# Spectral block with 128-row x2 tiles, column tiles for 64-row leftovers, merged stores, a reordered tail and shared copies of v

## The chip, the cores and the metric

The kernel runs on one core of one Trainium2 chip. The metric is device time in microseconds (us), taken from the execution on the chip; lower is better.

Names used below: PE is TensorE's matmul, PEld its weight load, DVE VectorE, ACT ScalarE, POOL GpSimd, SP SyncE, which only issues DMAs here. "L785" is line 785 of the kernel that the profile belongs to. The lines move between versions, so the tile names (out, num, x, dft, qpt) are what to hold on to.

## The reference

Two blocks in a row, batch 8, 576 positions, 8 heads of 64. The first is a linear attention with a cosine reweighting; the second projects to three branches, filters one of them along the sequence with a Fourier transform, gates, and projects back:

```python
def _attn_ref(q, k, v):                 # 8 x 8 x 576 x 64 each
    c, s = cos(pi/2 * pos/S), sin(pi/2 * pos/S)
    q_p = concat([relu(q)*c, relu(q)*s]);  k_p = concat([relu(k)*c, relu(k)*s])
    kv  = einsum('bhsf,bhsd->bhfd', k_p, v);  z = k_p.sum(axis=2)
    num = einsum('bhsf,bhfd->bhsd', q_p, kv)
    den = einsum('bhsf,bhf->bhs', q_p, z)[..., None] + 1e-06
    return num / den

def _moe_ref(x, w_proj, filter_fft, w_out):        # x: 8 x 576 x 512
    x1, x2, x3 = split(x @ w_proj, 3)
    y = x1 * irfft(rfft(x2, axis=1) * rfft(filter_fft, axis=0), n=S, axis=1) * x3
    return y @ w_out                               # 8 x 576 x 512, float32
```

(cut and shortened; `...` calls are numpy's.)

## The kernel before

It handles one batch after the other, software-pipelined: while PE finishes batch b's spectral part, DVE and ACT prepare batch b+1's q and k.

The projection x2 and the forward transform work in blocks of 96 rows:

```python
def emit_x2(b, bls=range(3)):
    ...
    for bl in bls:
        u = unit(f"x2_{b}_{bl}")
        for comp in range(2):
            for c in range(NC):                      # NC = 4
                nc.tensor.matmul(u[0:NP, comp],      # NP = 96
                    fx[:, c, ds(comp * 6 + 2 * bl, 2)].rearrange("p a b -> p (a b)"),
                    wp16[:, c, ds(DM, DM)], start=(c == 0), stop=(c == NC - 1))
        mark["x2f", b, bl] = nc.scalar.mul(out=x2f[:, bl], in_=u[0:NP], mul=X2SC)
# emit_dft: one matmul per (bl, comp) against tre / tim
```

The output has 576 rows in an order of 12 groups of 48: row k of group r lies at DRAM row 12k + r. It is computed in five tiles of 128 rows, and each piece of at most 48 rows of one group is one store, nearly all of them on SP's queue:

```python
OT = [0, 128, 256, 384, 448]
def emit_out(b, grps=OG):
    ov = out[b].rearrange("(k r) n -> r k n", r=12)
    ...
            while pos < hi_:
                m = pos // 48
                e = min(hi_, (m + 1) * 48)
                k0 = pos - m * 48
                r = 6 * (m % 2) + m // 2
                q_ = nc.sync
                if m % 2 == 1 and (last or (b == B - 2 and t > 1)):
                    q_ = nc.scalar if last else nc.gpsimd
                q_.dma_start(out=ov[r, k0 : k0 + e - pos], in_=sv[pos - OT[t] : e - OT[t]])
                pos = e
```

SP's queue also carries two kinds of DMA transpose: qp into qpt, which the matmul num uses as weights, and att into xt, which the gate matmuls of the spectral block use.

## Time and profile before

| | before |
|---|---|
| time, median of the 4 runs beside the changed kernel | 252.69 us (252.07 to 259.23) |
| profiled span | 252.0 us |
| start of the first of six full out groups | 90.53 us |
| five periods from there, to the last out start at 215.47 | 124.9 us |
| from there to the end | 36.5 us |

### The profile page before, as it was taken

Reading aid. Unit: us, or ns where it says so; the run is one execution under the profiler, and the core shown is the slowest. Engines: PE = TensorE matmul, PEld = TensorE weight load, DVE = VectorE, ACT = ScalarE, POOL = GpSimd, SP = SyncE. Lnnn points to the kernel's source line nnn. Section 1 sums busy time; section 2 is a strip of 40 time slices with the busy share of each in tenths; the row PEclk is TensorE's granted clock in tenths of the full one; section 3 lists DMA queues with packets and bytes.
Section 4 is the critical chain, followed back from the end, with each engine's and each line's share of the span. In section 5 each row is a group of like instructions: output and inputs, shape, how many; then the busy total and the mean of one; then the engine's idle time right before and its main releaser. Section 6 shows DMA issues by size and latency. Waiting matters only on the chain.

```text
span 252.0 us, 6140 instructions
## 1 busy us (share of the span) xinstructions
PE 226.1 (90%) x2313; PEld 159.9 (63%) x2313; DVE 210.4 (83%) x732; ACT 186.2 (74%) x281; POOL 38.1 (15%) x65
## 2 busy tenths in 40 slices
PE   0197897998988999999999999999999999999980
PEld 0067575655676867686768676867686778557730
DVE  7689899699779999999799979997998595828880
ACT  2244789799797876987698769876987488767720
POOL 8714211501501031103110311000000000000030
PEclk9997998899799999999999999999999999999996
DMA  5999999799999969999999999999982512153054
GB/s 68 167 205 205 207 200 153 101 166 196 173 121 157 169 56 202 174 176 194 200 225 143 141 217 199 137 183 156 161 197 53 153 41 58 44 146 83 3 153 140
DMA packets 74926, 37.30 MB, mean 148 GB/s; under 512 B 54288, under 2 KB 70160, under 8 KB 74896
## 3 DMA queue, kind: packets, MB, share of 16 engines
q0 software_dynamic: 26176, 17.21, 51.3%
q1 hardware_dynamic: 48320, 19.11, 40.6%
q10 hardware_dynamic: 400, 0.59, 0.7%
q8 instruction: 18, 0.29, 0.5%
q14 instruction: 12, 0.10, 0.2%
HBM read 33.69 MB, written 9.44 MB: 171 GB/s over the span
## 4 chain that ended last, share of the span: by engine, by line
PE 73%; DVE 13%; ACT 7%; DMA 3%; issue 1%; POOL 1%; POOLq 0%; DVEq 0%; ACTq 0%
PE x L674 21%; PE x L634 17%; PE out L752 12%; PE kv L527 5%; PE num L568 4%; PE fx L595 4%; PE dft L649 3%; DMA vraw<-in_v_dram 3%; PE inv L711 2%; PE inv L710 2%; DVE kp L104 2%; ACT va L142 1%; DVE eo L725 1%; DVE att L578 1%; PE qt L547 1%
## 5 line engine op out<-in xcount | busy, mean ns | idle before, releaser
L674 PE MATMUL x<-xt,wp 128*128 128x288 f16 x512 | 68.1, 286 | 0.0
L674 PEld LDWEIGHTS <-wp 128*128 128x128 f16 x512 | 48.9, 98 | 13.9 <-issue 0.9
L634 PE MATMUL x<-wp,fx 128*96 128x512 f16 x192 | 48.1, 395 | 1.6 <-DVE qpt L553 1.6
L752 PE MATMUL out<-wo,y 128*128 128x512 f16 x160 | 36.0, 379 | 0.1
L639 ACT ACTIVATE x2f<-x 96x1024 f16<-96x1024 f32 x24 | 24.5, 1020 | 14.2 <-PE x L634 13.9
L634 PEld LDWEIGHTS <-fx 128*96 128x96 f16 x192 | 23.0, 127 | 16.7 <-issue 3.7
L142 ACT COPY va<-vraw 96x768 f16<-96x768 f16 x32 | 25.2, 831 | 9.2 <-DMA vraw<-in_v_dram 9.2
L578 DVE TENSOR_TENSOR att<-num,rcp 96x768 f16<-96x768 f32 x32 | 30.3, 948 | 0.2
L752 PEld LDWEIGHTS <-y 128*128 128x128 f16 x160 | 15.3, 97 | 17.7 <-DVE y L730 0.6
L527 PE MATMUL kv<-va,kp 96*128 96x65 f16 x384 | 16.6, 199 | 10.2 <-ACT va L142 8.4
L684 ACT CAST x3s<-x 128x576 f16<-128x576 f32 x32 | 20.5, 641 | 5.9 <-PE x L674 5.9
L759 ACT ACTIVATE os<-out 128x1024 f32<-128x1024 f32 (+1 forms) x21 | 17.7, 880 | 9.0 <-PE out L752 8.7
L610 ACT CAST fx<-fx 128x576 f16<-128x576 f32 x32 | 20.6, 645 | 4.9 <-PE fx L595 4.9
L651 ACT CAST xf<-dft 96x1024 f16<-96x1024 f32 x24 | 24.2, 1008 | 0.0
L527 PEld LDWEIGHTS <-kp 96*128 96x128 f16 x384 | 15.1, 101 | 13.6 <-DVE kp L104 11.3
L699 DVE TENSOR_TENSOR g<-x3s,x1s 128x288 f16<-128x288 f16 x64 | 17.2, 299 | 6.8 <-ACT x3s L684 6.8
L681 ACT CAST x1s<-x 128x576 f16<-128x576 f32 x32 | 20.6, 645 | 1.8 <-PE x L674 0.8
L654 DVE TENSOR_TENSOR m<-xf,h 96x1024 f16<-96x1024 f16 x24 | 16.3, 681 | 6.1 <-ACT xf L651 5.1
L568 PEld LDWEIGHTS <-qpt 128*128 128x128 f16 (+1 forms) x384 | 16.2, 103 | 7.7 <-issue 3.9
L725 DVE TENSOR_TENSOR eo<-eq 128x288 f16<-128x288 f16 x64 | 17.5, 297 | 4.4 <-ACT eq L714 4.4
L595 PE MATMUL fx<-fm,att 96*128 96x96 f16 x240 | 17.0, 214 | 3.4 <-DVE att L578 1.7
L595 PEld LDWEIGHTS <-att 96*128 96x128 f16 x240 | 14.3, 101 | 7.6 <-DVE att L578 3.4
(192 smaller groups left out, 409.1 us busy)
## 6 DMA issues: line engine op xcount, KB each, us to landing
out_dram<-os SPq DMA_DIRECT2D x64, 96.0 KB, 2.2
kraw<-in_k_dram POOLq DMA_DIRECT2D x7, 576.0 KB, 8.6
vraw<-in_v_dram POOLq DMA_DIRECT2D x7, 576.0 KB, 8.9
qraw<-in_q_dram POOLq DMA_DIRECT2D x8, 288.0 KB, 6.0
qraw<-in_q_dram POOLq DMA_DIRECT2D x12, 144.0 KB, 5.9
wp<-in_moe_w_proj_dram POOLq DMA_DIRECT2D x3, 512.0 KB, 11.9
out_dram<-os SPq DMA_DIRECT2D x22, 64.0 KB, 2.2
out_dram<-os SPq DMA_DIRECT2D x23, 32.0 KB, 2.1
```

What stands on the lines that cost most here:

```text
L142: nc.scalar.copy(out=va_buf[b % 2][:, hs, :, 0:D], in_=raw_t[(b, "v")][:, hs].rearrange("p h (j d) -> p h j d", j=NJ),)
L527: nc.tensor.matmul(u[:, h // 4, ds((h % 4) * 65, 65)], kp[:, j, h].rearrange("p a b -> p (a b)"), va[:, h, j, 0:65], start=(j == 0), stop= ...
L568: nc.tensor.matmul(u[0:m, hh, ds(t * 65, 65)], qpt[:, c0 : c0 + 2 * m - 1 : 2], kvs[:, h // 4, ds((h % 4) * 65, 65)], start=True, stop=True,)
L578: mark["att", b, hp] = nc.vector.tensor_tensor(out=att[:, :, ds(hp * 128, 128)].rearrange("p t (h d) -> p h t d", h=2), in0=nv[:, :, :, 0: ...
L595: nc.tensor.matmul(dst.rearrange("p (g e o) -> p g e o", e=2, o=8)[:, :, e], att[:, 2 * j + e, ds(c * 128, 128)], fm[0:NP, gs], start=True ...
L610: mark["fx", b] = nc.scalar.copy(out=dst[:, c].rearrange("p g (j o) -> p j g o", j=3), in_=uf[:, 0:768].rearrange("p (j g o) -> p j g o", ...
L634: nc.tensor.matmul(u[0:NP, comp], fx[:, c, ds(comp * 6 + 2 * bl, 2)].rearrange("p a b -> p (a b)"), wp16[:, c, ds(DM, DM)], start=(c == 0) ...
L639: mark["x2f", b, bl] = nc.scalar.mul(out=x2f[:, bl], in_=u[0:NP], mul=X2SC)
L651: mark["xf", b, bl] = nc.scalar.copy(out=xf, in_=u[0:NP])
L674: nc.tensor.matmul(u[:, hf, 0:HS], wp16[:, i, ds(w * DM + c * 128, 128)], xt[:, i, ds(6 * hf, 6)].rearrange("p a b -> p (a b)") if b < DMA ...
L681: mark["x1s", b, c] = nc.scalar.copy(out=x1s, in_=us[0][:, :, 0:HS])
L752: nc.tensor.matmul(u[:, x], y[:, c, ds(OT[t], 128)], wo16[:, c], start=(c == 0), stop=(c == NC - 1),)
```

## The change

Its intent: fewer PE rows in x2 (three blocks of 96 rows and two components fit in four full tiles of 128 and a half one), the half tiles of x2 and out run as pairs of 64-column tiles side by side, two neighbouring groups of 48 output rows leave in one store of 96 rows, the last batch's work is reordered and its stores alternate between two queues, and half of the copies of v go from ACT to DVE at a later point. The core of the diff:

```diff
 # x2 and dft
-            for comp in range(2):
-                for c in range(NC):
-                    nc.tensor.matmul(u[0:NP, comp], fx[:, c, ds(comp * 6 + 2 * bl, 2)]..., ...)
+            if bl < 2:
+                for x in range(2):
+                    for c in range(NC):
+                        mm(u[:, x], 2 * bl + x, 128, c, range(NC))
+            else:
+                for c in range(2):
+                    for x in range(2):
+                        mm(u[ds(64 * x, 64), 0], 4, 64, c + 2 * x, range(2 * x, 2 * x + 2))
...
+    DFT = (
+        ((tre[:, 0], 0),), ((tpad[0], 0), (tpad[1], 1)), ((tpad[2], 1), (tpad[3], 2)),
+        ((tpad[4], 2),), ((tre[:, 2], 3),), ((tpad[5], 3), (tpad[6], 4)),
+    )
 # out
-        ov = out[b].rearrange("(k r) n -> r k n", r=12)
+        ov = out[b].rearrange("(k x y) n -> x y k n", x=2, y=6)
...
-                    e = min(hi_, (m + 1) * 48)
+                    e = pos + 96 if pos % 96 == 0 and pos + 96 <= hi_ else min(hi_, (m + 1) * 48)
                     q_ = nc.sync
-                    if m % 2 == 1 and (last or (b == B - 2 and t > 1)):
-                        q_ = nc.scalar if last else nc.gpsimd
+                    if last:
+                        q_ = (nc.sync, nc.scalar)[store[0] % 2]
+                    store[0] += 1
+                    if e - pos == 96:
+                        q_.dma_start(out=ov[:, m // 2], in_=sv[pos - OT[t] : e - OT[t]])
...
 # the loop over batches
-            for x in range(2):
-                with behind(*(("x2f", b, x) if b > 1 else ("kvs", 2))):
-                    emit_va(n + 1, (2 * x, 2 * x + 1))
+            ...
+                with behind("eo", b, 3):
+                    emit_va(n + 1, (0, 1))
+                with behind("g", b, 0):
+                    emit_va(n + 1, (2, 3), nc.vector.tensor_copy)
```

(cut: the padded tables' set-up, the 64-row tile of out, which goes as four pairs of 256-column halves, the last batch's accumulation order, the tail's order.) Three of a batch's stores become 96-row stores, 24 in all. Their place in DRAM is two runs of 48 rows.

More of the change, by code (lines that the diff above doesn't have):

```diff
@@ L83 @@
     tim = consts.tile([NP, 3, NP], FP16, tag="tim", name="tim")
+    tpad = [consts.tile([128, NP], FP16, tag=f"tpad{i}", name=f"tpad{i}") for i in range(7)]
     ire = consts.tile([NP, 4, QS], FP16, tag="ire", name="ire")
@@ L119 @@
     raw_t = {}
-    DMA_XT = 2
+    XT_DMA = (2, 3, 4, 5, 6, 7)
     DMA_QT = 2
@@ L137, in load_qk, with emit_va @@
             nc.gpsimd.dma_start(out=rw[:, hs], in_=view)
-    def emit_va(b, xs=range(4)):
+    def emit_va(b, xs=range(4), copy=nc.scalar.copy):
         for x in xs:
             hs = slice(2 * x, 2 * x + 2)
-            nc.scalar.copy(
+            copy(
                 out=va_buf[b % 2][:, hs, :, 0:D],
@@ L199, in emit_cols @@
         nc.vector.memset(warm, 0.0)
+        for t in tpad:
+            nc.vector.memset(t, 0.0)
         sj = cc["s6_i"]
@@ L279, in emit_fm @@
         nc.vector.tensor_tensor(out=ph, in0=ph, in1=rr, op=AL.subtract)
-        nc.scalar.activation(out=coef[:, 0:6], in_=ph, func=AF.Sin, scale=TWO_PI)
-        tsc(coef[:, 3:6:2], coef[:, 3:6:2], 1.0 / R3, AL.mult)
-        tsc(coef[:, 0:6], coef[:, 0:6], 2.0, AL.mult)
-        tsc(coef[:, 0:6], coef[:, 0:6], RC, AL.add, -RC, AL.add)
-        tsc(coef[:, 0:6], coef[:, 0:6], 0.5, AL.mult)
-        tsc(coef[:, 6:12], coef[:, 0:6], side, AL.mult)
+        cv = coef[:, 0:12].rearrange("p (b c s) -> p b c s", b=3, c=2)
+        c0, cb = cv[:, :, 0], cv[:, 1:3, 0, 1]
+        nc.scalar.activation(
+            out=c0, in_=ph.rearrange("p (b s) -> p b s", b=3), func=AF.Sin, scale=TWO_PI
+        )
+        tsc(cb, cb, 1.0 / R3, AL.mult)
+        tsc(c0, c0, 2.0, AL.mult)
+        tsc(c0, c0, RC, AL.add, -RC, AL.add)
+        tsc(c0, c0, 0.5, AL.mult)
+        tsc(cv[:, :, 1], c0, side, AL.mult)
         irow_i = cc["orow_i"][:, 0:6]
@@ L386, in emit_fwd_tables @@
             nc.vector.tensor_tensor(out=tb[:, 0], in0=tb[:, 0], in1=mask, op=AL.mult)
+        for i, to, tb, bl, lo, n in (
+            (0, 96, tim, 0, 0, 32), (1, 0, tim, 0, 32, 64), (2, 64, tre, 1, 0, 64),
+            (3, 0, tre, 1, 64, 32), (4, 32, tim, 1, 0, 96), (5, 96, tim, 2, 0, 32),
+            (6, 0, tim, 2, 32, 64), (6, 64, tim, 2, 32, 64),
+        ):
+            nc.sync.dma_start(out=tpad[i][to : to + n], in_=tb[lo : lo + n, bl])
     def emit_inv_turns():
@@ L588, in emit_fx @@
             fx_t[b] = work.tile([128, NC, 12, 48], FP16, tag="fx", bufs=2, name=f"fx{b}")
-            if b < DMA_XT:
+            if b not in XT_DMA:
                 xt_t[b] = work.tile([128, NC, 12, 48], FP16, tag="xt", bufs=2, name=f"xt{b}")
@@ L601, in emit_fx @@
             for dst, gs in ((fx, slice(0, 12)), (xt_t.get(b), slice(12, 24))):
-                if gs.start and b >= DMA_XT:
+                if gs.start and b in XT_DMA:
                     continue
@@ L627, in emit_x2, with mm @@
         if 0 in bls:
-            moe.setdefault(b, {})["x2f"] = work.tile([NP, 3, 2, DM], FP16, tag="x2f", name=f"x2f{b}")
+            moe.setdefault(b, {})["x2f"] = work.tile([128, 5, DM], FP16, tag="x2f", name=f"x2f{b}")
         x2f = moe[b]["x2f"]
+        def mm(dst, ch, n, c, cs):
+            nc.tensor.matmul(
+                dst, fx[:, c].rearrange("p g o -> p (g o)")[:, ds(128 * ch, n)],
+                wp16[:, c, ds(DM, DM)], start=(c == cs[0]), stop=(c == cs[-1]),
+            )
         for bl in bls:
             u = unit(f"x2_{b}_{bl}")
-            for comp in range(2):
-                for c in range(NC):
-                    nc.tensor.matmul(
-                        u[0:NP, comp],
-                        fx[:, c, ds(comp * 6 + 2 * bl, 2)].rearrange("p a b -> p (a b)"),
-                        wp16[:, c, ds(DM, DM)], start=(c == 0), stop=(c == NC - 1),
-                    )
-            mark["x2f", b, bl] = nc.scalar.mul(out=x2f[:, bl], in_=u[0:NP], mul=X2SC)
+            if bl < 2:
[6 more added lines that the diff above has]
+                        mm(u[ds(64 * x, 64), 0], 4, 64, c + 2 * x, range(2 * x, 2 * x + 2))
+            n = 2 if bl < 2 else 1
+            mark["x2f", b, bl] = nc.scalar.mul(
+                out=x2f[:, 2 * bl : 2 * bl + n], in_=u[:, 0:n], mul=X2SC
+            )
     def emit_dft(b, bls=range(3)):
@@ L647, in emit_dft @@
             u = unit(f"dft{b}_{bl}")
-            for comp, tab in ((0, tre), (1, tim)):
-                nc.tensor.matmul(u[0:NP, comp], tab[:, bl], x2f[:, bl, comp], start=True, stop=True)
+            for comp in range(2):
+                mm = DFT[2 * bl + comp]
+                for x, (tab, ch) in enumerate(mm):
+                    nc.tensor.matmul(
+                        u[0:NP, comp], tab, x2f[0 : tab.shape[0], ch],
+                        start=(x == 0), stop=(x == len(mm) - 1),
+                    )
             xf = work.tile([NP, 2, DM], FP16, tag="xf", bufs=2, name=f"xf{b}_{bl}")
@@ L659, in emit_dft @@
             mark["yf", b, bl] = nc.vector.tensor_tensor(out=yf[:, bl, 1], in0=m1[:, 1], in1=m2[:, 0], op=AL.add)
+    DFT = (
+        ((tre[:, 0], 0),), ((tpad[0], 0), (tpad[1], 1)), ((tpad[2], 1), (tpad[3], 2)),
+        ((tpad[4], 2),), ((tre[:, 2], 3),), ((tpad[5], 3), (tpad[6], 4)),
+    )
     X3_ACT = (0, 1, 2, 3)
@@ L676, in emit_gate @@
                         xt[:, i, ds(6 * hf, 6)].rearrange("p a b -> p (a b)")
-                        if b < DMA_XT else xt[:, :, i, ds(48 * hf, 48)],
+                        if b not in XT_DMA else xt[:, :, i, ds(48 * hf, 48)],
                         start=(i == 0), stop=(i == NC - 1),
@@ L687, in emit_gate @@
         for hf in range(2):
-            if b < DMA_XT:
+            if b not in XT_DMA:
                 gv = (g[:, c, 0:HS] if hf == 0 else g[:, c, HS:S][:, ::-1]).rearrange(
@@ L730, in emit_y @@
         nc.vector.tensor_tensor(out=y[:, c], in0=y[:, c], in1=g[:, c], op=AL.mult)
-    OT = [0, 128, 256, 384, 448]
+    OT = [0, 128, 256, 384, 512]
+    store = [0]
+    OGL = ((1, 0), (2, 4), (3,))
     OG = ((0, 1), (2, 3), (4,))
@@ L740, in emit_out, with mm @@
             u = unit(f"out{b}_{grp[0]}")
-            os_ = {}
+            os_, us = {}, {}
+            def mm(t, c, nr):
+                nc.tensor.matmul(
+                    us[t], y[:, c, ds(OT[t], nr)], wo16[:, c],
+                    start=(c == 0), stop=(c == NC - 1),
+                )
             for x, t in enumerate(grp):
@@ L747, in emit_out @@
                     os_[t] = late["p"].tile(
-                        [128, ng, DM], FP32, tag="osl" if last else f"os{ng}", bufs=5 if last else ng,
+                        [128, ng, DM // 2 if t == 4 and not last else DM], FP32, tag="osl" if last else f"os{ng}", bufs=5 if last else ng,
                         name=f"os{b}_{t}",
                     )
-                for c in range(NC):
-                    nc.tensor.matmul(
-                        u[:, x], y[:, c, ds(OT[t], 128)], wo16[:, c],
-                        start=(c == 0), stop=(c == NC - 1),
-                    )
-                if last:
-                    tsc(os_[t][:, 0], u[:, x], OUTSC, AL.mult)
-            if not last:
+                if t == 4 and not last:
+                    for c in range(NC):
+                        for hf in range(2):
+                            nc.tensor.matmul(
+                                u[ds(64 * hf, 64), x, 0 : DM // 2], y[:, c, 512:576],
+                                wo16[:, c, ds(hf * (DM // 2), DM // 2)],
+                                start=(c == 0), stop=(c == NC - 1),
+                            )
+                    nc.scalar.mul(
+                        out=os_[t][:, 0, 0 : DM // 2], in_=u[:, x, 0 : DM // 2], mul=OUTSC
+                    )
+                    continue
+                nr = 64 if t == 4 else 128
+                us[t] = u[0:nr, 0 if last else x]
+                part = range(NC)
+                if last and grp[0] == 1:
+                    part = range(NC - 1)
+                for c in part:
+                    mm(t, c, nr)
+                if last and len(part) == NC:
+                    nv = DM if t == 4 else DM // 2
+                    tsc(os_[t][0:nr, 0, 0:nv], us[t][:, 0:nv], OUTSC, AL.mult)
+                    if nv < DM:
+                        nc.scalar.mul(out=os_[t][0:nr, 0, nv:DM], in_=us[t][:, nv:DM], mul=OUTSC)
+            if last and grp[0] == 1:
+                for t in grp:
+                    mm(t, NC - 1, 128)
+                    tsc(os_[t][:, 0], us[t], OUTSC, AL.mult)
+            if not last and grp[0] < 4:
                 nc.scalar.mul(out=os_[grp[0]], in_=u[:, 0 : len(grp)], mul=OUTSC)
@@ L761, in emit_out @@
                 sv = os_[t][:, 0] if last else os_[grp[0]][:, x]
-                lo, hi_ = (OT[t], OT[t] + 128) if t < 4 else (512, 576)
-                pos = lo
+                pos, hi_ = (128 * t, 128 * t + 128) if t < 4 else (512, 576)
                 while pos < hi_:
-                    m = pos // 48
-                    e = min(hi_, (m + 1) * 48)
-                    k0 = pos - m * 48
-                    r = 6 * (m % 2) + m // 2
+                    m, k0 = pos // 48, pos % 48
+                    e = pos + 96 if pos % 96 == 0 and pos + 96 <= hi_ else min(hi_, (m + 1) * 48)
                     q_ = nc.sync
-                    if m % 2 == 1 and (last or (b == B - 2 and t > 1)):
-                        q_ = nc.scalar if last else nc.gpsimd
-                    q_.dma_start(out=ov[r, k0 : k0 + e - pos], in_=sv[pos - OT[t] : e - OT[t]])
+                    if last:
[3 more added lines that the diff above has]
+                        q_.dma_start(out=ov[:, m // 2], in_=sv[pos - OT[t] : e - OT[t]])
+                    elif t < 4 or last:
+                        q_.dma_start(
+                            out=ov[m % 2, m // 2, k0 : k0 + e - pos], in_=sv[pos - OT[t] : e - OT[t]]
+                        )
+                    else:
+                        for hf in range(2):
+                            q_.dma_start(
+                                out=ov[m % 2, m // 2, k0 : k0 + e - pos, ds(hf * (DM // 2), DM // 2)],
+                                in_=sv[64 * hf + pos - 512 : 64 * hf + e - 512, 0 : DM // 2],
+                            )
                     pos = e
@@ L880 @@
             emit_num(n, 3)
-            emit_xt(n)
+            if n in XT_DMA:
+                emit_xt(n)
         if b == 1:
@@ L889 @@
             emit_out(b - 1, OG[0:1])
+            emit_dft(b, (2,))
+            emit_out(b - 1, OG[1:2])
         for c in range(NC):
-            if b == B - 1 and c == NC - 1:
+            if b == B - 1 and c == 2:
                 for x in range(NC):
@@ L895 @@
                 emit_gate(b, c)
-                if c == 0:
+                if c == 0 and b < B - 1:
                     emit_dft(b, (2,))
@@ L908 @@
                 emit_qt(n + 1, x)
-            with behind("att", n, 1):
+            with behind(*("att", n, 3)):
                 emit_phi(n + 1, "k")
-            for x in range(2):
-                with behind(*(("x2f", b, x) if b > 1 else ("kvs", 2))):
-                    emit_va(n + 1, (2 * x, 2 * x + 1))
+            if b == 1:
+                with behind("kvs", 2):
+                    emit_va(n + 1)
+            else:
+                with behind("eo", b, 3):
+                    emit_va(n + 1, (0, 1))
+                with behind("g", b, 0):
+                    emit_va(n + 1, (2, 3), nc.vector.tensor_copy)
         for x in range(4):
-            if b >= 1 and x < 3 and (b != B - 1 or x > 0):
-                emit_out(b - 1, (OG[x],))
+            if b >= 1 and x < 3 and (b != B - 1 or x > 1):
+                emit_out(b - 1, ((OG if b < B else OGL)[x],))
         if n + 1 < B:
```

## The prediction

> **What bounds the kernel now.** I read the page's busy shares and slices first, to see which engine is full and when.
>
> ```profile
> PE 226.1 (90%) x2313; PEld 159.9 (63%) x2313; DVE 210.4 (83%) x732; ACT 186.2 (74%) x281; POOL 38.1 (15%) x65
> PE   0197897998988999999999999999999999999980
> DVE  7689899699779999999799979997998595828880
> ```
>
> A slice is 6.3 us. PE is at 9 tenths in every slice from about 80 us to 245 us; before that there are gaps, and DVE and ACT alternate as the bound. A busy PE need not be a bound PE, so next the chain of work that ended last, in order of time, for one batch in the middle:
>
> ```profile
> 140.58 4.32 PE out L752 x20
> 144.90 1.53 PE kv L527 x48
> 146.42 1.74 PE x L634 x8
> 148.16 0.79 PE num L568 x24
> 148.96 1.74 PE x L634 x8
> 151.09 0.45 PE dft L649 x2
> 151.94 1.75 PE x L634 x8
> 153.69 0.43 PE dft L649 x2
> 154.13 2.10 PE x L674 x16
> 165.59 4.32 PE out L752 x20
> ```
>
> The whole period is PE, and nothing is waited for: out starts at 90.53, 115.56, 140.58, 165.59, 190.62, so a batch takes 25.0 us. From it come the unit prices: a matmul of 512 columns costs 0.2175 us in x2 (1.74/8), 0.216 in out (4.32/20) and in dft. The table of stretches says how far the other engines are from that limit (PE, PEld, DVE, ACT, POOL busy):
>
> ```profile
> 140.58:165.59 25.01, 25.01 (x267) 17.99 (x266) 22.82 (x73) 20.78 (x32) 1.88 (x3) 1.00 1.22 178
> ```
>
> DVE has only 2.2 us of air per batch; the DMA share of 1.22 says that its queues are full too. The end is different. After PE's last matmul (the eviction that waits for it starts at 245.06) the span runs 6.9 us more, to 252.0:
>
> ```profile
> 240.66 7.85 SPq L772 DMA_DIRECT2D out_dram<-os  x12
> 241.18 3.35 PEld L752 LDWEIGHTS <-y 128*128 128x128 f16 x17 [0.59 <-DVE y L730]
> 242.33 5.86 ACTq L772 DMA_DIRECT2D out_dram<-os  x7
> 245.06 0.69 DVE L102 TENSOR_SCALAR os<-out 128x512 f32<-128x512 f32 x1 [0.17 <-PE out L752]
> ```
>
> Here the store queues set the end: 12 issues at about 0.65 us each on SP run until 248.5, and the last ones still have to land. PE also waited 0.59 us for DVE's last y.
>
> [...] No matmul of the kernel before runs as a concurrent pair, so the trace can't confirm the overlap. [...]
>
> ```profile
> 54.58 0.81 PE L465 MATMUL h_ps<-filt,hb 96*96 96x512 f16 x3
> 55.32 0.81 PE L478 MATMUL h_nyq<-feo,alt 96*1 96x512 f16 x3
> 56.06 0.42 PE L649 MATMUL dft<-x2f,tre 96*96 96x512 f16 x1
> ```
>
> Three matmuls at 0.216 would put h_nyq at 55.23 and dft at 55.97; both start 0.09 later. So I charge 0.1 us per switch, 0.2 for each visit to column mode. [...] the 96x1536 relu of q takes 573 ns and the 96x512 f16 copy of h 311 ns, so 1024 more elements cost 262 ns. A 96x768 copy of v on DVE is then about 0.38 us (estimate), against 0.83 on ACT.
>
> **The change part by part**, per batch.
>
> x2: 24 matmuls of 96 rows become 16 of 128 rows plus 4 of 64 rows in column tiles, as two pairs. 24 x 0.2175 = 5.22; after, 16 x 0.2175 = 3.48, the pairs 2 x 0.2175 = 0.44 if they overlap fully, the visit 0.2: 4.12. Gain 1.10.
>
> dft: a 96-row block now lies across two 128-row tiles in three of six cases, so 6 matmuls become 9 against zero-padded tables: 3 x 0.216 = 0.65 lost.
>
> out: the last 64 rows were done with 128 stationary columns, half of them repeated: 4 matmuls, 0.86. Now 8 of 256 columns in four pairs, 4 x 0.11 (half of 0.216), plus 0.2: 0.64. Gain 0.22.
>
> PE sum: -1.10 + 0.65 - 0.22 = -0.67, so the period should go from 25.0 to about 24.35.
>
> ACT: the third x2f eviction shrinks from 128x1024-like 1.02 to 128x512 (0.59, the price of the 128x512 os), the small os from 0.59 to about 0.37 (kvs of 128x260), and two of four v copies leave (2 x 0.83): 2.3 us less of 20.8. ACT is not on the path, so this pays nothing directly, but no PE wait on x2f should appear. DVE: two copies more, 0.7 us: 22.8 becomes 23.5 of 24.35. They stand before the last g, where DVE sat idle 0.57 for x3s, so most of it fills air. The instruction order also shows that all four att now come ahead of kp, which frees num's PSUM earlier.
>
> Setup up to 62 us: seven memsets on DVE and eight small table copies on SP lie beside the first loads; ACT is the chain at 48 to 63 us, and the shorter x2f takes 0.4 off it.
>
> Tail: x2, dft and out of the last batches give another 0.67; the last 64-row tile pays a visit (0.2) with no partner. The inverse now comes before the last two gates, and the first three of four accumulation steps of the first two out tiles run before y's last quarter is needed, so the 0.59 wait should go: in sum about -1.0. Stores: out of batch 6 is moved forward, and 96-row pieces leave 10 stores for the last batch, alternating between two queues. They should keep pace with PE, so that only the last tile's chain is left: a half-width eviction on two engines about 0.5, landing 2.2 to 3.5 (the page's 2.2, ACT queue up to 3.9), about 1.0 of closing. That is 4.6 instead of 6.9: -2.3.
>
> Sum: five full periods 5 x 0.67 = 3.4; the stretch 62 to 90 us, which DVE and ACT bound in part, 0.5; setup 0.4; tail 1.0 + 2.3. Together -7.6, so 244.7. I add 0.5 for new small waits and say 245.2 us, 2.8% less.
>
> **The rivals.**
>
> DVE becomes the bound. For: 23.5 of 24.35 is 97%[...]. Against: y is used 20 us after it is made, and yf is ready 2.5 us before the inverse. A period of 24.8, in all 247.5.
>
> The column pairs don't overlap. Then x2 gains 0.67, out loses 0.2, and with dft at -0.65 the period stays at 25.2. Only the tail and setup pay: about 249.5. For: nothing in this trace shows a pair[...].
>
> The DMA becomes the bound. The transposes that feed num share SP's queue with the stores:
>
> ```profile
> 143.56 1.80 SPq L539 DMA_TRANSPOSE qpt<-qp  x1
> 151.38 0.56 PE L568 MATMUL num<-kvs,qpt 128*128 128x65 f16 x12
> ```
>
> This one takes 7.2 us from issue to landing, so it is there at 150.8, 0.6 us before use. Stores of a batch fall only from 15 to 14 issues, the bytes stay. If DMA holds its pace and PE runs ahead, each of two or three periods gets a wait of 0.5 to 1 us on num: about 247. Against: the later copies of v delay the next load of v, so the transposes meet one load less, and after 165 us the loads are over.
>
> Fully hidden switches would go the other way: 0.4 us per batch more, about 242.5.
>
> **Range and chances.** The centre needs overlapping pairs, which I give 80%; DVE and DMA together cost 1 to 2 us in perhaps a third of cases; the tail is uncertain by 1 us either way. 242 to 248.8 should hold it 8 times in 10. 2% is 247.2: faster 0.78, within 0.21, slower 0.01.
>
> **What would show it.** Right: out-to-out distance near 24.35; the two halves of an x2 pair starting within a few tens of ns; gaps near 0.1 on either side of them; dft three at a time in 0.65; no PE wait for DVE or DMA in mid-kernel; DVE near 23.5 per period; v copies near 0.38 on DVE; last matmul to end about 4.6. Wrong: pairs 0.216 apart, num waiting for qpt, PE waiting for att or y, or stores still queueing 2 us behind the last eviction.

That pairs of 64-column matmuls overlap was the assumption; nothing in the trace of the kernel before shows it. A switch is the change from matmuls of 96 or 128 stationary columns to narrower ones, and back; its price is an estimate from the 0.09 us that the trace shows before and after the matmuls of h_nyq, which have one stationary column, and what passes in that time is not shown. The first rival's 24.8 us held an assumed slow rate for the copies of v on DVE. The half-width eviction at about 0.5 and the closing at about 1.0 were guesses: the changed kernel has 0.38 us for the first on ACT and 0.42 on DVE, and its last store's data end about 1.5 us before its span does.

## More of the kernel before

The prediction shows the rows of the page, the chain and the table of stretches. Two things more are needed to compare with. First the chain's shares by engine, from the page: which engine the end was waiting for.

```profile
PE 73%; DVE 13%; ACT 7%; DMA 3%; issue 1%; POOL 1%; POOLq 0%; DVEq 0%; ACTq 0%
```

DMA is 3% of it, nearly all in the first loads. Then the page's list of DMA issues for the output (how many, KB each, and the median time from issue to landing in us):

```profile
out_dram<-os SPq DMA_DIRECT2D x64, 96.0 KB, 2.2
...
out_dram<-os SPq DMA_DIRECT2D x23, 32.0 KB, 2.1
```

A row of output is 2 KB, so these are pieces of 48 and of 16 rows, and they land in about the same time.

## The result, and the profile after

The changed kernel took 286.1 us (median of 4 runs, 285.39 to 288.42) beside 252.69 for the kernel before. The ratio is 1.1347, 95% interval 1.1256 to 1.1439: slower by 13%, where 3% faster had been predicted. (A ratio here is the mean time of one kernel's fast runs over that of the other's fast runs of the same rounds, so it is not quite the ratio of the medians quoted.) Executions over 1.5% slower than the fastest of the same kernel are left out of the means.

The page of the changed kernel, its busy shares, PE's slices, the granted clock in the same slices, and the chain's shares by engine. A slice is now 7.1 us.

```profile
PE 228.3 (80%) x2333; PEld 154.4 (54%) x2333; DVE 212.8 (75%) x747; ACT 178.9 (63%) x275; POOL 35.3 (12%) x61
PE   0388979989799999932999699928999999959800
PEclk9999988989999999985699979998999999997965
PE 53%; DMA 22%; DVE 11%; ACT 7%; issue 1%; ACTq 1%; POOL 0%; SPq 0%; POOLq 0%
```

PE is not much busier than before (228.3 against 226.1 us); it is idle more. There are holes in the middle, at about 125, 160 and 188 us, a smaller one at about 252, and the end is empty. The clock falls to 0.50 within the first of them, at 126.5 us, and within 0.7 us of the end of the next three, at 164.0, 191.3 and 256.2 (`--windows`). And 22% of the chain is now DMA, against 3%. The list of waits names it (engine, line waited for: us in all, times, longest):

```profile
PE num L584 <- DMA qpt<-qp: 18.9, 5, 9.9
ACT os L829 <- DMA out_dram<-os: 5.6, 1, 5.6
```

PE's wait is for the transposes of q. ACT's is near the end of the kernel, at 249 to 254 us: it can't evict the next output before an earlier one has been stored, and PE then waits 3.3 us for ACT. The chain of work that ended last, from one batch to the next, in order of time (start, length, what), shows how the first of these waits looks:

```profile
112.97 3.46 PE out L785 x16
...
118.61 1.73 PE x L648 x8
120.34 0.24 PE num L584 x8
120.58 13.18 DMA qpt<-qp
133.81 0.89 PE num L584 x12
134.70 0.99 PE x L648 x4
135.69 1.45 PE dft L680 x3
```

That transpose, issued at 120.58, landed 13.2 us later. PE had other work for the first 3.3 us of that and then waited 9.9 us. The prediction had shown one that took 7.2 us and landed 0.6 us ahead of its use. Why it was issued so late shows in SP's timeline just before (start, length of the issue, line, count):

```profile
95.71 4.21 SPq L842 DMA_DIRECT2D out_dram<-os  x2
102.56 12.15 SPq L555 DMA_TRANSPOSE qpt<-qp  x3
114.80 5.68 SPq L633 DMA_TRANSPOSE xt<-att  x1
120.58 4.88 SPq L555 DMA_TRANSPOSE qpt<-qp  x1
```

In the kernel before, the same issues for the same batch read:

```profile
101.99 9.39 SPq L539 DMA_TRANSPOSE qpt<-qp  x3
111.47 4.82 SPq L617 DMA_TRANSPOSE xt<-att  x1
116.38 1.42 SPq L539 DMA_TRANSPOSE qpt<-qp  x1
```

So these issues are slow in both kernels. Behind the merged stores they took 22.9 us of SP's time from the first to the end of the last, in place of 15.8, and the last went out 4.2 us later. The next table of stretches puts a good period beside a bad one (us; PE, PEld, DVE, ACT, POOL busy; clock, DMA share, GB/s):

```profile
88.76:112.97 24.21, 24.21 (x270) 17.09 (x269) 24.04 (x77) 17.87 (x28) 3.54 (x5) 1.00 0.96 116
112.97:150.19 37.22, 27.34 (x271) 18.30 (x269) 24.14 (x76) 19.21 (x30) 3.54 (x5) 0.82 1.09 141
```

The first is what the prediction wanted: 24.21 us, all PE, better than the 24.35 it named. The second is 13.0 us longer: 9.9 us of waiting for qpt, and 3.1 us in which PE was busy longer with the same work, because its clock was lower afterwards (the four x matmuls of the column pairs took 0.99 us above, at a granted clock of 0.50; undisturbed, at 1.00, they take 0.55). `--windows` in steps of half a microsecond shows two levels of the granted clock here, 1.00 and 0.50. After the wait of 9.9 us it stood at 0.50 for another 6.3 us of work, until about 140.1. In the next period a wait of 2.4 us was followed by 0.50 from about 164.0 to 167.4. So here the low clock lasted 3.4 us after the shorter wait, and 6.3 us after the longer.

The same count over three stretches of the whole span, from the chain's out starts:

| | before | after | difference |
|---|---|---|---|
| to the first out | 90.53 | 88.76 | -1.8 |
| five periods | 124.9 | 146.8 | +21.8 |
| last out start to the end | 36.5 | 49.5 | +12.9 |
| span | 252.0 | 285.0 | +33.0 |

Two of the five periods took 24.21; the other three took 37.22, 28.36 and 32.78, together 25.7 above that. Of these, 18.9 are the waits for qpt and 6.8 the longer busy time of PE (27.34 + 25.99 + 26.12 - 3 x 24.21). The end is a second matter. PE's last matmul is done about 269.5, the last store is issued at 271.37, and the kernel ends at 285.0. The DMA view of the stretch from 272.5 to 282 us (busy tenths of the 16 engines, and GB/s, in 40 slices):

```profile
DMA  4665332111112210011111111111111111111111
GB/s 86 121 138 112 112 95 78 52 43 52 52 52 52 17 17 0 17 35 52 52 52 43 52 52 52 52 52 52 52 52 43 52 52 52 52 52 52 52 52 52
```

`--windows` from 277 to 282 gives a DMA share of 0.13 and 51 GB/s: 0.13 of sixteen engines is 2.1, so about two engines are at work, while nothing else is left to do. The merged store's pattern in DRAM is 2 x 48, so its outer dimension is 2. That this is what leaves the store with two engines was the guess; nothing up to here shows it. The prediction doesn't look at the pattern. Whether the guess is right is what the experiments test.

### The profile page after: what moved, and what is told of

It reads as the page before. It is cut to its first block, busy times and chain, and to the rows that moved or that the text cites. A ratio compares the mean times of both kernels' runs of the same rounds, so it can differ in the third digit from the quotient of the medians.

```text
span 285.0 us, 6190 instructions
## 1 busy us (share of the span) xinstructions
PE 228.3 (80%) x2333; PEld 154.4 (54%) x2333; DVE 212.8 (75%) x747; ACT 178.9 (63%) x275; POOL 35.3 (12%) x61
## 4 chain that ended last, share of the span: by engine, by line
PE 53%; DMA 22%; DVE 11%; ACT 7%; issue 1%; ACTq 1%; POOL 0%; SPq 0%; POOLq 0%
PE x L713 19%; DMA qpt<-qp 14%; PE x L648 8%; PE out L785 7%; DMA out_dram<-os 5%; PE dft L680 4%; PE kv L543 3%; PE inv L749 3%; PE inv L750 3%; PE fx L611 3%; PE num L584 2%; DMA vraw<-in_v_dram 2%; DVE kp L107 2%; DVE att L594 2%; ACT va L145 1%
## 5 line engine op out<-in xcount | busy, mean ns | idle before, releaser
L713 PE MATMUL x<-xt,wp 128*128 128x288 f16 x512 | 69.9, 292 | 3.4 <-ACT os L829 3.3
L666 ACT ACTIVATE x2f<-x 128x1024 f16<-128x1024 f32 (+1 forms) x24 | 21.1, 881 | 40.6 <-PE x L648 40.6
L648 PE MATMUL x<-wp,fx 128*128 128x512 f16 (+1 forms) x160 | 39.8, 420 | 2.1 <-DVE qpt L569 1.6
L584 PE MATMUL num<-kvs,qpt 128*128 128x65 f16 (+1 forms) x384 | 17.9, 201 | 21.0 <-DMA qpt<-qp 18.9
L785 PE MATMUL out<-wo,y 128*128 128x512 f16 (+1 forms) x132 | 30.3, 379 | 0.0
L590 DVE TENSOR_TENSOR rcp<-num,epsc 96x12 f32<-96x12 f32 x32 | 5.2, 163 | 27.5 <-PE num L584 27.4
L543 PE MATMUL kv<-va,kp 96*128 96x65 f16 x384 | 16.5, 198 | 10.0 <-ACT va L145 8.2
L145 ACT COPY va<-vraw 96x768 f16<-96x768 f16 x24 | 18.7, 845 | 9.0 <-DMA vraw<-in_v_dram 9.0
L648 PEld LDWEIGHTS <-fx 128*128 128x128 f16 (+1 forms) x160 | 13.8, 107 | 16.9 <-issue 6.3
L785 PEld LDWEIGHTS <-y 128*128 128x128 f16 (+1 forms) x132 | 12.4, 98 | 14.6 <-issue 1.0
L829 ACT ACTIVATE os<-out 128x1024 f32<-128x1024 f32 x14 | 14.3, 1032 | 8.6 <-DMA out_dram<-os 5.6
## 6 DMA issues: line engine op xcount, KB each, us to landing
kraw<-in_k_dram POOLq DMA_DIRECT2D x7, 576.0 KB, 12.4
```

The lines of the kernel that those rows point to most:

```text
L145: copy(out=va_buf[b % 2][:, hs, :, 0:D], in_=raw_t[(b, "v")][:, hs].rearrange("p h (j d) -> p h j d", j=NJ),)
L543: nc.tensor.matmul(u[:, h // 4, ds((h % 4) * 65, 65)], kp[:, j, h].rearrange("p a b -> p (a b)"), va[:, h, j, 0:65], start=(j == 0), stop= ...
L584: nc.tensor.matmul(u[0:m, hh, ds(t * 65, 65)], qpt[:, c0 : c0 + 2 * m - 1 : 2], kvs[:, h // 4, ds((h % 4) * 65, 65)], start=True, stop=True,)
L648: nc.tensor.matmul(dst, fx[:, c].rearrange("p g o -> p (g o)")[:, ds(128 * ch, n)], wp16[:, c, ds(DM, DM)], start=(c == cs[0]), stop=(c == ...
L666: mark["x2f", b, bl] = nc.scalar.mul(out=x2f[:, 2 * bl : 2 * bl + n], in_=u[:, 0:n], mul=X2SC)
L713: nc.tensor.matmul(u[:, hf, 0:HS], wp16[:, i, ds(w * DM + c * 128, 128)], xt[:, i, ds(6 * hf, 6)].rearrange("p a b -> p (a b)") if b not i ...
```

## The experiments

Theory: the merged store goes to two engines because of its outer dimension of 2, takes several times longer, and holds up what comes behind it. Rivals: it is the size of the store; it is its three-dimensional pattern; or something else in the change (order of the transposes, column tiles, later copies) makes num wait. Each ratio is to the kernel before. The times quoted are medians of all runs; where two versions are subtracted, the means of their fast runs are used, and that is said.

### fix48: the changed kernel without merged stores

```diff
-                    e = pos + 96 if pos % 96 == 0 and pos + 96 <= hi_ else min(hi_, (m + 1) * 48)
+                    e = min(hi_, (m + 1) * 48)
```

> The changed kernel with each 96-row store made as two 48-row stores again; all else of the change stays. Theory S (few engines): a 96-row store has the slowest dimension 2 on the DRAM side and is carried by 2 of the 16 DMA engines; everything queued behind it waits. Then this run loses the whole regression: 245 us (242 to 248), PE not waiting for qpt, tail from last matmul to end about 5 us. Rival L (late loads): the v copies on DVE delay the loads of v, which then meet the transposes; then it stays at 280 us or more. Rival O (new order of the tail and of att and kp): stays above 265.

Measured: 246.38 us (243.91 to 248.77), ratio 0.9765 [0.9656, 0.9873]. One line gives back 40 us, and the other parts of the change are a gain. It has 17 store issues on SP per batch, more than either kernel, and no wait of num for qpt. Its chain in the place shown above:

```profile
111.52 3.46 PE out L785 x16
...
118.89 0.80 PE num L584 x24
119.69 1.73 PE x L648 x8
```

All 24 num matmuls run at once. This kernel beats both others; to know by how much, it ran again in five rounds.

> The version with 48-row stores once more, in five rounds, since three rounds gave 0.9765 with an interval that reached past 2%: a ratio of 0.97 to 0.985, 246 to 248 us; nothing else is at stake than the size.

Measured: 245.7 us (243.07 to 253.16), beside 253.09 for the kernel before; 0.9711 [0.9644, 0.9779]: faster, 2.9%.

### before_merged: the kernel before with only the merged stores

```diff
-        ov = out[b].rearrange("(k r) n -> r k n", r=12)
+        ov = out[b].rearrange("(k x y) n -> x y k n", x=2, y=6)
-                    e = min(hi_, (m + 1) * 48)
+                    e = pos + 96 if pos % 96 == 0 and pos + 96 <= hi_ else min(hi_, (m + 1) * 48)
+                    dst = ov[:, m // 2] if e - pos == 96 else ov[m % 2, m // 2, k0 : k0 + e - pos]
```

> The kernel before with only the 96-row stores of the change (24 of them, in place of 48 stores of 48 rows). Theory S: about the whole regression appears here too, 275 to 295 us, PE waiting for qpt. Rivals L and O: 252 us, or a little faster for fewer issues.

Measured: 294.11 us (290.5 to 295.79), ratio 1.1648 [1.1515, 1.1781]. Merging costs 16% here, and 16% in the changed kernel (1.1347 / 0.9765 = 1.162). Together with fix48 this fixes the cause on the merged stores, alone and undone. (Its profiled run was a slow one, so no line of it is quoted.)

One thing these edits did not hold still. SP's timelines show that the order in which SP issues a batch's transposes moved with the stores, though no edit touched it. The kernel before, the changed kernel and merge_mid issue three of qpt, then xt, then the fourth of qpt; fix48, both cuts below, merge_last, x2_nocol and fix48_va_act issue xt and then four of qpt; before_merged and merge_mid_pool four of qpt and then xt. The kernel before and fix48, with 48-row stores, have the first and the second of these orders, and in neither does num wait for qpt, so the order alone is not the cause. How much of the mid-kernel cost it carries once the stores are slow was not tested. The pair of cuts below and the pair fix48 and merge_last each share one order, so their differences are free of it.

### before_cut34 and before_cut32: the kernel before, its 48-row stores cut in two

To tell engines from size and pattern, small plain stores with an awkward row count. The author expected few engines for 34 rows (micro, below, shows a DMA share of 0.13 for such a store, about two engines) and more for 32 and 16 (their shares were not taken). Both versions issue equally many stores.

```diff
-                    q_.dma_start(out=ov[r, k0 : k0 + e - pos], in_=sv[pos - OT[t] : e - OT[t]])
+                    for lo_, hi2 in ((0, 34), (34, 48)) if e - pos == 48 else ((0, e - pos),):
+                        q_.dma_start(out=ov[r, k0 + lo_ : k0 + hi2],
+                                     in_=sv[pos - OT[t] + lo_ : pos - OT[t] + hi2])
```

(before_cut32: 32 in place of 34.)

> The kernel before; each 48-row store is made as one of 34 rows and one of 14. Nothing is merged, all stores are smaller, the DRAM access pattern is plain. [...] 34 rows go over 2 engines, so it is slow, 270 to 295 us, with the same bytes (5 MB) on two engines as in the changed kernel (4.5 MB). If instead the three-dimensional pattern or the size of a store is the trouble: no slower than the control cut at 32, within 2 us.

> Control for the cut at 34: the same number of stores, cut at 32 (32 and 16 rows[...]). Theory S: only the 9 more issues per batch cost, 252 to 257 us; far below the cut at 34. If issues are the trouble, both cuts are equally slow.

Measured: 285.4 us (283.22 to 288.6), ratio 1.132 [1.1213, 1.1427], for 34 + 14, and 267.17 us (264.67 to 269.99), ratio 1.0591 [1.0474, 1.0708], for 32 + 16. Two rows more in one store and two fewer in the other cost 18 us. No store is larger than before and none has a third dimension. The waits of before_cut34 have the form of the changed kernel's:

```profile
PE num L568 <- DMA qpt<-qp: 16.5, 4, 8.6
```

The control missed its expectation: 14.5 us for nine more issues per batch on SP, which I had taken as nearly free. Its profiled run was slow, so I don't take its waits apart; but that more issues ahead of the transposes cost time is measured, and it means that the idea of saving issues was not empty. It was the way of saving them that failed.

### micro: the stores by themselves

A kernel that only stores. Its output is wrong, which doesn't matter for the time. One tile is filled by a memset, stored, and filled again, so each memset waits for the store before it.

```diff
+    nc.sync.dma_start(out=half[0, r], in_=os_[0:48])           # 48 rows
+    nc.sync.dma_start(out=half[1, r, 0:32], in_=os_[0:32])
+    nc.sync.dma_start(out=half[2, r, 0:34], in_=os_[0:34])
+    nc.sync.dma_start(out=half[3, r, 0:47], in_=os_[0:47])
+    nc.sync.dma_start(out=one[4, r], in_=os_[0:96])            # 96 rows, one even step
+    nc.sync.dma_start(out=two[5, :, r], in_=os_[0:96])         # 96 rows as 2 x 48
+    nc.scalar.dma_start(out=two[6, :, r], in_=os_[0:96])
+    nc.gpsimd.dma_start(out=two[7, :, r], in_=os_[0:96])
```

> The stores alone (a wrong result on purpose): each store is awaited by a memset of its tile before the next goes out, three rounds of eight forms, all with rows of 2 KB. Theory S with a rate of 26 GB/s per engine (52 GB/s at 2 of 16 engines, as in the changed kernel's tail) on top of about 2 us: 48 rows 2 us, 32 rows 2, 96 rows at one even step 2 to 2.5, against 34 rows (2 engines) 4.5, 47 rows (1 engine) 5.5, 96 rows as 2x48 about 5.5 us, on SP and on ACT's queue alike. On GpSimd's queue it may differ. Rival Z (size of the store): 96 rows even is as slow as 2x48. Rival P (the three-dimensional pattern itself): 34 and 47 rows are as fast as 48.

Its timeline, second of three rounds (start, length, the memset, and in brackets how long DVE waited before it, and for what), cut to the memsets after the stores of 48, 47, 96 and 2 x 48 rows:

```profile
45.16 0.48 DVE L31 MEMSET os<- 128x512 f32 x1 [2.17 <-DMA out_dram<-os]
...
57.90 0.48 DVE L31 MEMSET os<- 128x512 f32 x1 [6.35 <-DMA out_dram<-os]
60.72 0.48 DVE L31 MEMSET os<- 128x512 f32 x1 [2.33 <-DMA out_dram<-os]
68.11 0.48 DVE L31 MEMSET os<- 128x512 f32 x1 [6.91 <-DMA out_dram<-os]
```

All of that round (the three rounds agree within 0.1 us, GpSimd's store within 0.5):

| store | DMA share in its midst | engines by that share | rows for each | waited, us |
|---|---|---|---|---|
| 48 rows | not taken | | | 2.17 |
| 32 rows | not taken | | | 1.85 |
| 34 rows | 0.13 | 2 | 17 | 3.08 |
| 47 rows | 0.06 | 1 | 47 | 6.35 |
| 96 rows, even step | up to 0.82 | about 13 | about 7 | 2.33 |
| 2 x 48, SP's queue | 0.13 | 2 | 48 | 6.91 |
| 2 x 48, ACT's queue | not taken | | | 6.89 |
| 2 x 48, GpSimd's queue | not taken | | | 8.08 |

96 rows with one even step take hardly longer than 48 (2.33 us against 2.17): size falls. 47 rows in a plain two-dimensional pattern are nearly as slow as 2 x 48 (6.35 against 6.91): the pattern's third dimension falls. The wait rises with the rows per engine: from 34 to 47 rows, 30 rows more on an engine cost 3.27 us, 0.109 each, and by that price (an estimate from these two waits) 2 x 48 should take 6.46; it takes 6.91. The times expected were off (4.5 for 34 rows, 5.5 for 47 and for 2 x 48); their order is the theory's. The number of engines isn't in the timeline, but the table of stretches gives it, in the midst of the stores of 34, 47 and 2 x 48 rows (DVE and POOL busy, clock, DMA share, GB/s):

```profile
48.80:50.30 1.50, 0.00 (x0) 0.00 (x0) 1.00 0.13 38
53.20:56.00 2.80, 0.00 (x0) 0.00 (x0) 1.00 0.06 18
63.50:66.50 3.00, 0.00 (x0) 0.00 (x0) 1.00 0.13 39
```

The DMA share is the mean over 16 engines: 0.13 of 16 is two engines (2.1), 0.06 is one (1.0). In the store of 96 rows with an even step it reaches 0.82 (59.2 to 60.0), about 13 engines. So by these shares the same 96 rows have two engines as 2 x 48 and about 13 with one even step. What sets the number for other shapes and row counts was not shown.

### merge_last and merge_mid: the merged stores in the last batch only, or in all but the last

```diff
 # merge_last                                            (merge_mid: `not last`)
-                    e = min(hi_, (m + 1) * 48)
+                    e = pos + 96 if last and pos % 96 == 0 and pos + 96 <= hi_ else min(hi_, (m + 1) * 48)
```

> The repaired kernel (all stores of 48 rows or fewer) with the 96-row stores put back in the last batch alone: 3 of 24. If the harm is only a longer last landing plus the queue of three such stores on two engines (3 x 3.8 us from 235 us on), the time goes up by 6 to 8 us to 253; the other 30 us or more of the regression then belong to the seven batches before. If the tail were the whole harm, 280.

> The changed kernel with the merged 96-row stores in batches 0 to 6 only; the last batch stores 48 rows at a time. Theory (waits of num behind slow stores are one cost, the slow tail another, and the two add): 246.4 for the version without merged stores plus about 29 us of num waits gives 272 to 279 us, with 15 to 19 us of PE wait on qpt, several pieces of 10 us or more of DMA in the chain between 110 and 210 us, and a tail after the last matmul near 5 us. Rival (the stores of the last batch are slow mainly because the earlier ones still sit in their engines): the tail stays above 10 us here too, and the time is above 281.

Measured: merge_last 257.3 us (254.69 to 261.71), ratio 1.0145 [1.0067, 1.0223]; merge_mid 274.78 us (270.62 to 278.36), ratio 1.0796 [1.0684, 1.0907]. By the means of the fast runs, three stores in the last batch cost 10.9 us over fix48's 245.6, more than the 6 to 8 expected from 3.8 us a store, an estimate from 192 KB at the tail's 52 GB/s (merge_last ran on another chip than fix48; the kernel before took 253.19 and 252.69 there); the other twenty-one cost 27.0. The two nearly add up: 245.6 + 10.9 + 27.0 = 283.5, and the changed kernel took 286.5. In merge_last no num waits for qpt and the periods stay at 24.2. merge_mid has the waits (16.5 us), and it ends 5.7 us after its last matmul, so the rival that the early stores slow the last ones falls.

Why three stores cost 11 us is worth a sum. In the changed kernel they are issued at 268.04, 269.69 and 271.37. Alone each takes 6.9 us, of which about 2 are there even for 32 rows (1.85 in micro). If one pair of engines carries all three one after the other, each for the other 4.9 us, the last ends at 268.04 + 3 x 4.9 + 2 = 284.7 (an estimate from the micro run). The end was 285.0. By this sum, that two queues issue them doesn't help.

### merge_mid_pool: the merged stores of batches 0 to 6 on GpSimd's queue

Does a transpose wait because it stands behind the stores in SP's queue, or because it needs the same engines? The same transfers from another queue tell the two apart.

```diff
-                        q_.dma_start(out=ov[:, m // 2], in_=sv[pos - OT[t] : e - OT[t]])
+                        nc.gpsimd.dma_start(out=ov[:, m // 2], in_=sv[pos - OT[t] : e - OT[t]])
```

> As merge_mid, but the merged stores of batches 0 to 6 are issued by GpSimd's queue and no longer by SP's; the same transfers, the same bytes. Theory A (what waits is the order in SP's queue: a transpose isn't issued until the stores ahead of it have gone): the waits of num on qpt fall from 15 to 19 us to under 4, and the time to 247 to 256, unless the loads of q, k and v, which GpSimd issues too, come late; then va, kp or qp wait instead of num. Rival B ([...] the two that carry the stores hold them up, whichever queue the stores came from): num still waits over 10 us and the time stays above 268.

Measured: 260.67 us (257.25 to 271.27), ratio 1.0217 [1.0132, 1.0302], between the two expectations. num doesn't wait for qpt any more, as theory A said, but another transpose is late in its place. It is the one that SP now issues last: xt stands behind all four of qpt here, which was not so in merge_mid.

```profile
PE x L713 <- DMA xt<-att: 9.0, 2, 6.2
```

And most other transfers are slower than in fix48. From the DMA view of both between 100 and 160 us (KB each, and the median us to landing), first fix48:

```profile
kraw<-in_k_dram POOLq DMA_DIRECT2D x2, 576.0 KB, 9.4
qpt<-qp SPq DMA_TRANSPOSE x12, 4.0
xt<-att SPq DMA_TRANSPOSE x3, 6.2
```

Then merge_mid_pool:

```profile
kraw<-in_k_dram POOLq DMA_DIRECT2D x2, 576.0 KB, 17.3
qpt<-qp SPq DMA_TRANSPOSE x8, 9.0
xt<-att SPq DMA_TRANSPOSE x2, 14.8
```

By the means of the fast runs, leaving SP's queue takes back 14.6 of the 27.0 us, and the other 12.4 remain, with transposes that share no queue with the merged stores landing more than twice as late. That this is the shared engines is the likely reading. It isn't fully shown: GpSimd also issues the loads, which here start at other times, and the order of the transposes changed as well.

### x2_nocol: no column pairs in x2

The last 64 rows as four matmuls of 128 stationary columns, half of them repeated, with zeros in the table for the repeated half (that line is cut below). The base is fix48.

```diff
-                for c in range(2):
-                    for x in range(2):
-                        mm(u[ds(64 * x, 64), 0], 4, 64, c + 2 * x, range(2 * x, 2 * x + 2))
+                for c in range(NC):
+                    nc.tensor.matmul(u[:, 0], fx[:, c].rearrange("p g o -> p (g o)")[:, ds(448, 128)],
+                                     wp16[:, c, ds(DM, DM)], start=(c == 0), stop=(c == NC - 1))
```

> The repaired kernel with the last 64 rows of x2 done by four matmuls of 128 stationary columns (half of them repeated rows), no column tile in x2. If the pairs overlap, the third x2 block goes from 0.55 to 0.85 us and a period from 24.21 to 24.5; over 7 batches plus 2 us, 248. If they do not overlap: no change.

Measured: 247.52 us (243.85 to 249.44), ratio 0.9784 [0.9718, 0.9851], not to be told from fix48. The period shows more: 24.39 against 24.21 us. fix48's chain has, for x2's pairs and what follows them:

```profile
147.09 0.55 PE x L648 x4
147.64 0.78 PE dft L680 x3
```

Three dft matmuls take 0.65 elsewhere in the same period, so 0.13 of the 0.78 comes with their place right after the pairs. In x2_nocol the same two groups take 0.86 and 0.65. Four matmuls in two pairs take 0.55 us where four plain ones take 0.86, so pairs do overlap, and gain 0.86 + 0.65 - 0.55 - 0.78 = 0.18 us a batch.

### fix48_va_act: all copies of v on ACT, at their old place

```diff
-                with behind("eo", b, 3):
-                    emit_va(n + 1, (0, 1))
-                with behind("g", b, 0):
-                    emit_va(n + 1, (2, 3), nc.vector.tensor_copy)
+                for x in range(2):
+                    with behind("x2f", b, x):
+                        emit_va(n + 1, (2 * x, 2 * x + 1))
```

> The repaired kernel with the copies of v all on ACT, placed where the kernel before had them. The prediction says that ACT's relief pays nothing directly: PE-bound, within 1 us of the repaired kernel. Rival: the placing of the copies (DVE at 24.0 of 24.2 us per period, later loads of v) matters; then 3 us or more either way.

Measured: 251.16 us (248.12 to 253.06), ratio 0.9863 [0.9801, 0.9926]; fix48 has 0.9711. The copies' place and engine together are worth about 4 us (1.5% of 253). This run moved both at once. Its trace speaks for the place: PE waits 3.8 us for qpt, where fix48 has no such wait, and qpt is back in the chain twice:

```profile
114.74 9.55 DMA qpt<-qp
...
143.18 9.07 DMA qpt<-qp
```

Early copies free v's buffer early, and its next load is then issued at 104.17 us, just ahead of the transposes at 105.76, whose four issues take 12.8 us; in fix48 that load starts at 110.67 and the four take 6.8. The copies decide when a load may start, and the load meets the transposes.

## Why the prediction was wrong, point by point

**The step that failed** is the price of the stores. The prediction says that "96-row pieces leave 10 stores for the last batch" that "should keep pace with PE", with a landing of 2.2 to 3.5 us, and of the DMA rival that "Stores of a batch fall only from 15 to 14 issues, the bytes stay". It counted issues and bytes and took the landing from stores of 48 rows. In place of 2.2 us a merged store takes 6.9, where 96 rows with one even step take 2.3 (micro): the difference is the DRAM pattern that starts with a dimension of 2. That one term adds 10.9 us at the end (merge_last over fix48), where -2.3 had been forecast, and 27.0 in mid-kernel (merge_mid), where nothing had been charged but 0.5 for "new small waits". The count was off too: the last batch has 12 stores in the trace, six on each queue, not 10; that is small beside it.

**The rival was the right one and too small.** "num waiting for qpt" is what happened. The prediction sized it at 0.5 to 1 us in two or three periods; three periods lost 13.0, 4.2 and 8.6 us. A transpose that came 0.6 us before its use has no room for a store that takes 4.7 us longer. The low clock after each wait, which the prediction didn't consider, added 6.8 us.

**The PE step was right.** The period was to fall by 0.67 to 24.35; undisturbed it is 24.21, in the changed kernel and in fix48. x2 with its pair: 2 x 1.73 + 0.55 + 0.13 = 4.14, predicted 4.12. dft: 9 matmuls, 0.65 more, as predicted. out: 3.46 + 0.56, and 0.10 more in the kv after it (1.63 against 1.53), 4.12, predicted 4.32 - 0.22 = 4.10. The 0.14 that were not foreseen lie in the first gate group, 1.96 us against 2.10; its cause was not looked for. The rival that the pairs don't overlap falls.

**DVE and ACT**: DVE was to need 23.5 us of a period; fix48's table of stretches has 23.54.

```profile
135.73:159.94 24.21, 24.21 (x270) 17.09 (x269) 23.54 (x75) 19.16 (x30) 3.54 (x5) 1.00 1.16 201
```

A copy of v on DVE takes 0.348 us (estimated 0.38), so that rival falls as well. ACT has 19.2 where 18.5 was predicted.

**The copies of v** were said to pay "nothing directly". They pay about 4 us, by the argument that the prediction put under its third rival: "the later copies of v delay the next load of v, so the transposes meet one load less". The mechanism was there, and its size was missing.

**Setup and tail** without the merged stores: to the first out 90.53 became 87.31, 3.2 us where 0.9 was predicted; the last stretch 36.5 became 33.7, 2.8 where 3.3 was; fix48 ends 5.0 us after its last matmul, predicted 4.6. With five periods at 0.78 (3.9), fix48's profiled span is 9.9 us shorter than before's, and its median 7.4 us; predicted were 7.1. So without the merged stores the sum is about right, in part by luck: setup gave more than it had in it, and without the moved copies the waits of fix48_va_act would have eaten half of the gain.

## What to carry to other kernels

Before merging DMAs, look at the outermost dimension of the pattern as the instruction carries it, and not only at bytes and issues: here a store of twice the size took three times as long in the shape 2 x 48 (6.91 us against 2.17), and hardly longer with one even step (2.33). Stores of this kind on two queues may still share their few engines, as the end of the changed kernel suggests (285.0 us, against 284.7 by the sum for one pair). Then ask what stands behind it. The profile's waits named a transpose and the chain named a transpose; the fault was in the store in front of it, and undoing one line at a time is what showed it. And when a buffer is freed, ask which transfer that starts and what it will meet.
